# A planned attention-and-long-convolution kernel: the first pair's shared keys apart, zero fills moved, the sine table first, and the last batch's dense units in two sets of banks

## The chip, the cores and the metric

The kernel runs on one core of one Trainium2 chip. The metric is the device time of one launch in microseconds (us), the median of several executions. Five engines work side by side, each in its own program order: TensorE (PE; its weight loads PEld), VectorE (DVE), ScalarE (ACT), GpSimd (POOL) and SyncE (SP), which here only issues DMA.

## What is computed

Eight batches of 448 positions, 12 heads of 64 channels; all inputs and the output are float32.

```python
# attention, with one more exp(-m) in the denominator ("off by one")
scores = q @ k.T / sqrt(64)
e = exp(scores - max); attn = e / (sum(e) + exp(-max) + 1e-9)
x = attn @ v                                   # -> (8, 448, 768), heads side by side
# gate and long convolution
x1, x2, x3 = split(x @ w_proj)                 # w_proj 768 x 2304
x2 = irfft(rfft(x2, axis=1) * rfft(filter, axis=0), n=448, axis=1)
out = (x1 * x2 * x3) @ w_out                   # 768 x 768
```

## The kernel before, in words

Work comes in 48 pairs of heads (six pairs to a batch; index g or i) and, per batch, a dense part. For each pair the keys and queries are turned so that channels lie on partitions, score tiles are made for four blocks of keys (t = 0 to 3), exponentials are taken on ScalarE (`exps`, L652), and the values are weighted (`attn_out`, L684: 28 matmuls in two halves) and normed on VectorE (`norm`, L706). Block 0 of a pair is its *shared* block: the last 64 keys of both heads, laid out as a block diagonal in the tile `ks`; it is made of `rests`, which one DMA loads for a whole batch. Blocks 1 to 3 hold the other keys of each head.

For batches 0 and 1 (`staged`, L300) SP loads keys, values and queries of each pair as float32 into slots of `nat`; the first pair's queries are loaded by ScalarE's queue. GpSimd casts them to bf16 (L343 keys, L349 queries, L356 values; pair 0's queries on VectorE), L372 casts the shared keys into `ks` (for batch 0 half on VectorE, half on GpSimd) and L377 the shared values into `vr`. Then `turn` (L380) transposes the shared block, three key blocks and four query blocks on TensorE into one PSUM bank, and `q_back` and `k_back` (L393, L401) copy the result to `qT` and `kT` on VectorE. Later batches (`loaded`, L418) are loaded and cast by GpSimd's queue and turned by DMA.

The weights are loaded by GpSimd's queue too: the three parts of `wproj_bf` (L626), the filter (L541) and `wout_bf` (L631), each when certain casts have been made (`GATES`, L210).

The dense part of a batch (`dense`, L768) consists of units, each of which fills a PSUM bank on TensorE and is copied out by ScalarE or VectorE:
- P (`proj2`, L822): the x2 projection, on folded x (`xf`), four groups pg by two column halves ch; 6 matmuls each.
- Z (`spectrum`, L849): its transform, two single matmuls per call; VectorE then multiplies with the filter's spectrum (`t`, L866; `yh`, L872).
- G (`gate`, L895): the x1 (part 0) and x3 (part 1) projections of six channel blocks dt, 6 matmuls each; part 0 is copied by ScalarE, part 1 multiplied with it by VectorE (`g`, L913).
- I (`inverse`, L933): the inverse transform of a channel block, 4 matmuls, copied by ScalarE (`cr`, L946); VectorE makes `cw`, `cv` and `yT` of two blocks (L955 to L981).
- O (`project`, L1003): the output projection, 6 matmuls for 128 rows and 384 columns. The first three are split, 4 matmuls on the first four channel blocks and 2 on the last two, so that they can begin before the last `yT` is made.

PSUM holds two score tiles of two banks each (ring `sc`), one attention output (`op`) and three single banks (ring `hy`), which all dense units, the turns and batch 0's shared scores use in turn.

The order on each engine is made by a planner (`Plan`, L42): each step is added with an engine, a cost, a wanted time, what it needs and makes, and which ring slots it takes and gives; `run` simulates the engines and emits each step when its model says that it can start. `after` is a time before which a step may not start in that model. So a changed need, cost or slot moves other steps too. At the start there are small steps of set-up: `spin` (L1087, 40 matmuls on the identity), the fills of `ks` and `vr` with zeros by ScalarE (`blank`, L1084), `phases` and `sines` (L493, L512), which make the tables of the transforms, a first exponential (L1098), and `turn`/`turn_back`, `ft`, `mirror`/`mirror_back` (L550 to L582), which derive the tables bt, ft and fr.

Of the kernel before, what the change touches and what calls it, by code (L numbers as in the profile page):

```python
# [183 lines left out]
def kernel(  # L184
# [21 lines left out]
    BPS = 7.4  # L206
    ZV = 8.0
    RE1 = 4.0
    FT = 7.0
# [90 lines left out]
    def staged(b):  # L300
# [3 lines left out]
        for hp in range(NHP):  # L304
# [62 lines left out]
            if hp == 0:  # L367
                for u in range(2):
                    c = slice(64 * u, 64 * u + 64)
                    on_pool = b > 0 or u == 1  # L370
                    add("POOL" if on_pool else "DVE", 0.55 if on_pool else 0.37, tau(g) - 5.9,
# [8 lines left out]
            def turn(g=g, hp=hp):  # L380
                T[g]["ps"] = tps = phy.tile([128, 512], F32, name="tps", tag="hy")
                tb = tps.bitcast(BF16)
                nc.tensor.transpose(tb[:, 0:128], ks[:, hp, :], ident_bf)
# [9 lines left out]
            def k_back(g=g, hp=hp):  # L393
                tb = T[g]["ps"].bitcast(BF16)
                to = kT[b % 2][:, hp].rearrange("p t c -> p (t c)")
                if g == NHP:
                    nc.scalar.copy(to, tb[:, 0:512])
                else:
                    nc.vector.tensor_copy(to, tb[:, 0:512])
# [8 lines left out]

            w = tau(g) - (3.5 if g else 6.0)
            hy = ("hy", ("T", g))  # L410
            add("PE", 0.45, w, turn, need=[("ck", g), ("cq", g), ("crk", b), "ident"], make=[("T", g)],
# [4 lines left out]
            add(back, 0.36, w + 0.2, k_back, need=[("T", g)] + old, make=[("kT", g)], give=[hy])  # L416
# [130 lines left out]
    def more_tables():  # L547
# [31 lines left out]
        add("PE", 0.25, 24.0, mirror, need=["ft", "half"], make=["rps"], take=[("hy", "rps")])  # L579
# [54 lines left out]
    T = {}  # L634

    def attention(i):
# [27 lines left out]
        for t in range(4):  # L664
            w = tau(i, t / 4)
            ring = "sc" if t or b else "hy"
            if t == 0 or b == 0:
                add("PE", 0.4 if t else 0.19, w, lambda t=t: scores(t),
                    need=[("kT", i), ("qT", i)] + ([("S", i - 1, 2)] if b else []),
# [98 lines left out]
    def dense(b):  # L768
# [5 lines left out]
        at = [0.0]  # L774
# [12 lines left out]
        def xT():  # L787
            return W["xT", b]

# [32 lines left out]
        def proj2(pg, ch):  # L822
            L["P", pg, ch] = pps = phy.tile([128, 512], F32, name="pps2", tag="hy")
# [17 lines left out]
        def P(pg, ch):  # L841
            hy = ("hy", ("P", b, pg, ch))
            w = span(0.97)
            add("PE", 0.975, w, lambda: proj2(pg, ch), need=[("xf", b, pg), ("w", 1)], make=[("P", b, pg, ch)],
# [4 lines left out]
        def spectrum(pg, ch):  # L849
            K = BLK_K[pg]  # L850
            L["Z", pg, ch] = xps = phy.tile([128, 512], F32, name="xsp", tag="hy")
# [25 lines left out]
        def Z(par, ch):  # L877
            xs = ("xs", (b, par, ch))
            for rs in range(2):
                pg = 2 * par + rs  # L880
                hy = ("hy", ("Z", b, pg, ch))
                w = span(0.16)
                add("PE", 0.165, w, lambda pg=pg: spectrum(pg, ch), need=[("x2", b, pg, ch), "ft", ("hrs", par)],
# [11 lines left out]
        def gate(dt, part):  # L895
            L["G", dt, part] = p = phy.tile([128, 512], F32, name="pps1", tag="hy")
# [18 lines left out]
        def G(dt, part):  # L915
            hy, x1 = ("hy", ("G", b, dt, part)), ("x1", (b, dt))
            w = span(1.13)
            add("PE", 1.135, w, lambda: gate(dt, part),
# [250 lines left out]
```

## Time and profile before

| | |
|---|---|
| median of 5 executions | 391.57 us (390.91 to 392.86) |
| profiled execution: own time, span | 391.33 us, 389.5 us |
| mean granted TensorE clock | 0.989 |
| exponentials `e` on ScalarE, 144 of 128x896 | 127.5 us, 924 ns each |
| gates, 576 matmuls of 128x448 (L898) | 121.8 us, 352 ns each |
| `P`, 384 matmuls of 113x384 (L825) | 70.5 us, 326-328 ns each |
| VectorE `g` (L913), 48 | 29.6 us, 616 ns each |
| table loads on ScalarE before 8 us | 3, 1.28 us each |
| `ks` and `vr` zero fills on ScalarE | 0.83 and 0.84 us |
| first scores on TensorE, first exponential | 8.26 us, 8.66 us |
| first P on TensorE | 36.30 us |
| last matmul's end, last copy's end | 384.77 us, 385.27 us |

Times inside a profile count from the start of the span. Matmuls overlap in the pipeline: 352 ns is what one takes from start to end, while the chain counts six of them as 1.14 us. A row of the order of time gives the start, the time taken, the engine, the line, the operation with its tiles, and in brackets how long the engine was idle before it and what ended that. A row of the chain gives start, time, engine and line of a piece of the chain that ended last. A row of the windows gives the stretch, its length, the busy time of PE, PEld, DVE, ACT and POOL, the granted TensorE clock, the DMA share and GB/s.

### The profile page before, as it was taken

The numbers are of one execution on the slowest core, as the hardware profiler recorded it, in microseconds if no ns is written. First come the engines' busy times: TensorE is split into PE (matmuls) and PEld (weight loads), VectorE is DVE, ScalarE is ACT, GpSimd is POOL, SyncE is SP. The second block draws the span as 40 slices with busy tenths as digits, with TensorE's granted clock in tenths as the row PEclk, the third lists the DMA queues.
The fourth block names the chain that finished last, engine by engine and source line by source line (L and its number), as shares of the span: only waits on it lengthen the run. The fifth ranks groups of instructions, "written<-read, shape, count | busy, mean of one in ns | idle before, by whom it ended". The sixth has DMA issues, their size and how long they took to land.

```text
span 389.5 us, 8980 instructions
## 1 busy us (share of the span) xinstructions
PE 373.1 (96%) x3461; PEld 233.8 (60%) x3461; DVE 271.5 (70%) x815; ACT 266.4 (68%) x461; POOL 112.8 (29%) x179
## 2 busy tenths in 40 slices
PE   6997999999999989999999999999999999999895
PEld 5664665656665566556755576556755576566552
DVE  5588769863987559956698449856798449955770
ACT  7797676737776847766876767866876768843443
POOL 7785418436340822331406222601100000000000
PEclk9699999999999999999999999999999999999999
DMA  8999999999999999799999899959831311021004
GB/s 201 245 232 236 223 207 146 154 138 210 144 141 135 234 140 125 98 112 168 137 118 93 156 153 166 86 81 175 116 56 29 140 37 29 15 94 43 0 3 162
DMA packets 179419, 50.44 MB, mean 129 GB/s; under 512 B 166125, under 2 KB 175792, under 8 KB 179376
## 3 DMA queue, kind: packets, MB, share of 16 engines
q0 software_dynamic: 101680, 17.80, 64.6%
q1 hardware_dynamic: 76768, 31.83, 41.6%
q8 instruction: 27, 0.44, 0.5%
q10 hardware_dynamic: 928, 0.23, 0.3%
q14 instruction: 16, 0.13, 0.2%
HBM read 43.86 MB, written 11.01 MB: 141 GB/s over the span
## 4 chain that ended last, share of the span: by engine, by line
PE 86%; DVE 7%; ACT 3%; issue 1%; DMA 1%; POOL 0%; SPq 0%; POOLq 0%; DVEq 0%; ACTq 0%
PE pps L898 27%; PE pps L825 16%; PE ops L1010 14%; PE op L698 9%; PE sc L648 8%; PE op L693 3%; PE cps L937 3%; PE xsp L852 2%; PE sc L650 2%; DMA rests<-in_k_dram 1%; DVE xb L713 1%; ACT e L656 1%; PE xps L747 1%; DVE xf L802 1%; DVE uw L593 1%
## 5 line engine op out<-in xcount | busy, mean ns | idle before, releaser
L656 ACT ACTIVATE e<-sc 128x896 bf16<-128x896 f32 x144 | 127.5, 924 | 17.6 <-PE sc L648 16.6
L898 PE MATMUL pps<-xT,wproj_bf 128*128 128x448 bf16 x576 | 121.8, 352 | 1.1 <-ACT xs L860 0.4
L898 PEld LDWEIGHTS <-wproj_bf 128*128 128x128 bf16 x576 | 52.0, 97 | 47.0 <-issue 7.7
L825 PE MATMUL pps<-wproj_bf,xf 128*113 128x384 bf16 x384 | 70.5, 328 | 0.9 <-ACT xs L860 0.6
L825 PEld LDWEIGHTS <-xf 128*113 128x113 bf16 x384 | 48.5, 132 | 16.6 <-issue 5.7
L698 PE MATMUL op<-vn,e 128*128 128x65 bf16 x1152 | 57.7, 195 | 0.1
L698 PEld LDWEIGHTS <-e 128*128 128x128 bf16 x1152 | 51.2, 98 | 5.6 <-ACT e L656 0.3
L1010 PE MATMUL ops<-wout_bf,yT 128*128 128x384 bf16 x288 | 51.8, 326 | 0.1
L1022 ACT COPY osb<-ops 128x384 f32<-128x384 f32 x56 | 25.9, 484 | 26.9 <-PE ops L1010 26.6
L693 PE MATMUL op<-vr,er 128*128 128x130 bf16 x192 | 42.5, 221 | 1.5 <-DVE xb L713 1.5
L713 DVE TENSOR_TENSOR xb<-op,rec 128x256 bf16<-128x256 f32 x96 | 40.7, 424 | 3.3
L435 POOL DMA_DIRECT2D nat<-in_k_dram x36 | 29.9, 850 | 43.7 <-DMA kT<-nat 42.1
L648 PE MATMUL sc<-qT,kT 64*128 64x448 bf16 x288 | 41.7, 360 | 0.6 <-ACT er L661 0.5
L711 DVE TENSOR_SCALAR rec<-op 128x4 f32<-128x4 f32 x96 | 15.2, 158 | 37.6 <-PE op L698 36.2
L866 DVE TENSOR_TENSOR t<-xs,hrs 113x768 bf16<-113x768 bf16 (+1 forms) x64 | 34.5, 554 | 8.0 <-ACT xs L860 7.8
L910 ACT CAST x<-pps 128x448 bf16<-128x448 f32 x48 | 26.2, 545 | 18.6 <-PE pps L898 17.5
L1010 PEld LDWEIGHTS <-yT 128*128 128x128 bf16 x288 | 26.5, 98 | 19.5 <-DVE yT L981 1.7
L661 ACT ACTIVATE er<-sc 128x448 bf16<-128x448 f32 x48 | 26.7, 557 | 14.3 <-PE sc L650 14.1
L913 DVE TENSOR_TENSOR g<-x,pps 128x448 bf16<-128x448 bf16 x48 | 29.6, 616 | 7.9 <-PE pps L898 7.6
L837 DVE CAST x<-pps 113x384 bf16<-113x384 f32 x32 | 17.8, 555 | 23.4 <-PE pps L825 23.4
L946 ACT CAST cr<-cps 128x452 bf16<-128x452 f32 x48 | 26.3, 549 | 11.4 <-PE cps L937 11.4
L860 ACT CAST xs<-xsp 113x384 bf16<-113x384 f32 (+1 forms) x64 | 28.0, 490 | 5.1 <-PE xsp L852 4.5
(103 smaller groups left out, 440.3 us busy)
## 6 DMA issues: line engine op xcount, KB each, us to landing
out_dram<-osb SPq DMA_DIRECT2D x24, 384.0 KB, 2.3
nat<-in_q_dram POOLq DMA_DIRECT2D x24, 168.0 KB, 5.7
vn<-in_v_dram POOLq DMA_DIRECT2D x6, 672.0 KB, 11.5
wproj_bf<-in_moe_w_proj_dram POOLq DMA_DIRECT2D x3, 1152.0 KB, 12.9
nat<-in_k_dram POOLq DMA_DIRECT2D x36, 96.0 KB, 4.7
nat<-in_q_dram SPq DMA_DIRECT2D x22, 112.0 KB, 5.2
nat<-in_k_dram SPq DMA_DIRECT2D x12, 192.0 KB, 4.5
nat<-in_v_dram SPq DMA_DIRECT2D x12, 192.0 KB, 4.5
```

The lines of the kernel that those rows point to most:

```text
L435: nc.gpsimd.dma_start(kn[:, :, 1 + t, c], kr[:, :, 4 * u + t, :])
L648: nc.tensor.matmul(sc[:, u, 0:S], kT[b % 2][c, hp, t, :], qT[b % 2][c, hp, :])
L656: nc.scalar.activation(e[:, 0 : 2 * S].rearrange("p (u n) -> p u n", u=2), sc[:, :, 0:S], AF.Exp, scale=SCALE)
L693: nc.tensor.matmul(op[:, n, :, :], e[0][:, o : o + 128], vr[b % 2][:, hp, :, :], start=True, stop=False)
L698: nc.tensor.matmul(op[:, n, u, :], e[1 + t][:, u * S + o : u * S + o + 128], vn[b % 2][:, hp, 4 * u + t, :], start=False, stop=(u == 1 and ...
L713: nc.vector.tensor_tensor(W["xb", b][:, hp, 2 * hf : 2 * hf + 2, :].rearrange("p t (u d) -> p t u d", u=2), op[:, :, :, 0:DH], rec[:].unsq ...
L825: nc.tensor.matmul(pps[:FQ, :DCH], W["xf", b][:, pg, kt, 0:FQ], wproj_bf[:, kt, D + ch * DCH : D + (ch + 1) * DCH], start=(kt == 0), stop= ...
L860: nc.scalar.copy(L["xs", par, ch][:K, pg % 2, :], L["Z", pg, ch][:K, :DCH])
L866: nc.vector.tensor_tensor(t[:K], L["xs", par, ch][:K], h, op=ALU.mult)
L898: nc.tensor.matmul(p[:, :S], wproj_bf[:, kt, 2 * part * D + dt * 128 : 2 * part * D + (dt + 1) * 128], xT()[:, kt, 0:S], start=(kt == 0), ...
L913: nc.vector.tensor_tensor(g[:, dt, :], L["x1", dt], p[:, :S], op=ALU.mult)
L1010: nc.tensor.matmul(ops[:n, :DCH], y[:, dt, 0:n], wout_bf[:, dt, ch * DCH : (ch + 1) * DCH], start=(dt == 0), stop=(dt == NDT - 1),)
```

## The change

Six edits, on lines of the kernel before:
- `turn` of pair 0 transposes only the three key and four query blocks; the shared block gets a `turn0` of its own, into its own bank, copied by VectorE (`back0`), while the other key blocks are copied by ScalarE. Pair 0's turn no longer needs the casts of `ks`, and pair 0's shared scores (t = 0) are wanted last of its four.
- The zero fills of `ks` and of `vr[0]` become memsets on VectorE, the second not before 7.4 in the planner's time.
- ScalarE starts with a sine on a dummy value, so that the sine table is loaded first.
- The planner's times for ft, bt (7.0 to 8.0, 7.4 to 8.2) and for `mirror` (24 to 29, and not before) are later.
- The cast of batch 0's shared keys is wanted at 3.0 instead of 0.1.
- In the last batch every other dense unit takes its bank from the score ring instead of the three single banks (`bank`, `room`); of a score tile's two banks one is used.

The planner's new order for these and neighbouring steps follows from that: mirror and the copies `fr` move from the first 12 us behind pair 5's attention, on GpSimd one value cast goes ahead of the first `wproj_bf` load and one cast of shared values behind it, and in the last batch one gate more stands before the first inverse.

```diff
@@ -203,10 +203,10 @@
     BASE2 = 77.0
     READY1 = 80.0
     READY0 = 34.0
-    BPS = 7.4
+    BPS = 8.2
     ZV = 8.0
     RE1 = 4.0
-    FT = 7.0
+    FT = 8.0
     GATES = (
         (1, [("iv", 5), ("ir", 1), ("ik", 7), ("iq", 7)]), ("F", [("cv", 8)]), (0, [("cv", 9)]), (2, [("cv", 10)]),
         ("O", [("cv", 11)]),
@@ -368,7 +368,7 @@
                 for u in range(2):
                     c = slice(64 * u, 64 * u + 64)
                     on_pool = b > 0 or u == 1
-                    add("POOL" if on_pool else "DVE", 0.55 if on_pool else 0.37, tau(g) - 5.9,
+                    add("POOL" if on_pool else "DVE", 0.55 if on_pool else 0.37, tau(g) - 5.9 if g else 3.0,
                         lambda c=c, on_pool=on_pool: (nc.gpsimd if on_pool else nc.vector).tensor_copy(
                             ks[c, :, c], rests[c, 0]
                         ),
@@ -380,7 +380,8 @@
             def turn(g=g, hp=hp):
                 T[g]["ps"] = tps = phy.tile([128, 512], F32, name="tps", tag="hy")
                 tb = tps.bitcast(BF16)
-                nc.tensor.transpose(tb[:, 0:128], ks[:, hp, :], ident_bf)
+                if g:
+                    nc.tensor.transpose(tb[:, 0:128], ks[:, hp, :], ident_bf)
                 for t in range(1, 4):
                     nc.tensor.transpose(
                         tb[:, t * 128 : (t + 1) * 128], T[g]["kn"][:, t - 1, :], ident_bf
@@ -395,8 +396,10 @@
                 to = kT[b % 2][:, hp].rearrange("p t c -> p (t c)")
                 if g == NHP:
                     nc.scalar.copy(to, tb[:, 0:512])
+                elif g:
+                    nc.vector.tensor_copy(to, tb[:, 0:512])
                 else:
-                    nc.vector.tensor_copy(to, tb[:, 0:512])
+                    nc.scalar.copy(to[:, 128:512], tb[:, 128:512])
 
             def q_back(g=g, hp=hp):
                 tb = T[g]["ps"].bitcast(BF16)
@@ -406,14 +409,25 @@
                 else:
                     nc.vector.tensor_copy(to, of)
 
+
+            def turn0():
+                T[0]["ps0"] = tps = phy.tile([128, 512], F32, name="tps0", tag="hy")
+                nc.tensor.transpose(tps.bitcast(BF16)[:, 0:128], ks[:, 0, :], ident_bf)
+
+            def back0():
+                nc.vector.tensor_copy(kT[0][:, 0, 0, :], T[0]["ps0"].bitcast(BF16)[:, 0:128])
+
+            if g == 0:
+                add("PE", 0.1, 2.0, turn0, need=[("crk", 0), "ident"], make=["T0"], take=[("hy", "T0")])
+                add("DVE", 0.2, 2.0, back0, need=["T0"], make=["kT0"], give=[("hy", "T0")])
             w = tau(g) - (3.5 if g else 6.0)
             hy = ("hy", ("T", g))
-            add("PE", 0.45, w, turn, need=[("ck", g), ("cq", g), ("crk", b), "ident"], make=[("T", g)],
+            add("PE", 0.45, w, turn, need=[("ck", g), ("cq", g), "ident"] + ([("crk", b)] if g else []), make=[("T", g)],
                 take=[hy], give=[("k0", g), ("q0", g)])
             old = [("S", g - 2 * NHP, 3)] if b >= 2 else []
             back = "ACT" if g == NHP else "DVE"
             add(back, 0.33, w + 0.1, q_back, need=[("T", g)] + old, make=[("qT", g)], give=[hy])
-            add(back, 0.36, w + 0.2, k_back, need=[("T", g)] + old, make=[("kT", g)], give=[hy])
+            add(back if g else "ACT", 0.36, w + 0.2, k_back, need=[("T", g)] + old, make=[("kT", g)], give=[hy])
 
     def loaded(b):
 
@@ -576,7 +590,7 @@
         add("DVE", 0.35, FT, after=FT, emit=lambda: nc.vector.tensor_scalar(
             ft[:], tab["sb"][:FQ, :, 0:FQ], tab["half"][:FQ, 0:1], None, op0=ALU.mult), need=["sines", "half"],
             make=["ft"])
-        add("PE", 0.25, 24.0, mirror, need=["ft", "half"], make=["rps"], take=[("hy", "rps")])
+        add("PE", 0.25, 29.0, mirror, need=["ft", "half"], make=["rps"], take=[("hy", "rps")], after=29.0)
         add("ACT", 0.9, 25.0, mirror_back, need=["rps"], make=["fr"], take=[("yR", "fr")], give=[("hy", "rps")])
         add("PE", 0.25, BPS, turn, need=["ident", "sines"], make=["bps"], take=[("hy", "bps")], after=BPS)
         add("DVE", 0.7, BPS, turn_back, need=["bps", "half"], make=["bt"], give=[("hy", "bps")])
@@ -662,11 +676,11 @@
 
         P["scores"] = scores
         for t in range(4):
-            w = tau(i, t / 4)
+            w = tau(i, t / 4 if i or t else 1.0)
             ring = "sc" if t or b else "hy"
             if t == 0 or b == 0:
                 add("PE", 0.4 if t else 0.19, w, lambda t=t: scores(t),
-                    need=[("kT", i), ("qT", i)] + ([("S", i - 1, 2)] if b else []),
+                    need=[("kT", i), ("qT", i)] + ([("S", i - 1, 2)] if b else []) + ([] if i or t else ["kT0"]),
                     make=[("S", i, t)], take=[(ring, ("S", i, t))])
             elif (3 * i + t) % 2 == 0:
 
...
@@ -786,6 +800,17 @@
 
         def xT():
             return W["xT", b]
+
+        def bank(key):
+
+            if b == n_batches - 1:
+                at[1] += 1
+            return ("sc" if at[1] % 2 else "hy", key)
+
+        def room(hy, name):
+            if hy[0] == "hy":
+                return phy.tile([128, 512], F32, name=name, tag="hy")
+            return psc.tile([128, 2, 512], F32, name="sc")[:, 0, :]
 
 
         def first(ds, n):
...
@@ -839,16 +864,16 @@
                 nc.scalar.copy(to, of)
 
         def P(pg, ch):
-            hy = ("hy", ("P", b, pg, ch))
+            hy = bank(("P", b, pg, ch))
             w = span(0.97)
-            add("PE", 0.975, w, lambda: proj2(pg, ch), need=[("xf", b, pg), ("w", 1)], make=[("P", b, pg, ch)],
+            add("PE", 0.975, w, lambda: proj2(pg, ch, hy), need=[("xf", b, pg), ("w", 1)], make=[("P", b, pg, ch)],
                 take=[hy], give=[("xf", b)])
             add(("ACT", "DVE")[ch], (0.38, 0.47)[ch], w, lambda: proj2_back(pg, ch), need=[("P", b, pg, ch)],
                 make=[("x2", b, pg, ch)], take=[("x2", b)], give=[hy])
 
-        def spectrum(pg, ch):
+        def spectrum(pg, ch, hy):
             K = BLK_K[pg]
-            L["Z", pg, ch] = xps = phy.tile([128, 512], F32, name="xsp", tag="hy")
+            L["Z", pg, ch] = xps = room(hy, "xsp")
             nc.tensor.matmul(
                 xps[:K, :DCH], ft[:, pg, :K], W["x2", b][:, pg, ch * DCH : (ch + 1) * DCH]
             )
...
@@ -913,9 +938,9 @@
                 nc.vector.tensor_tensor(g[:, dt, :], L["x1", dt], p[:, :S], op=ALU.mult)
 
         def G(dt, part):
-            hy, x1 = ("hy", ("G", b, dt, part)), ("x1", (b, dt))
+            hy, x1 = bank(("G", b, dt, part)), ("x1", (b, dt))
             w = span(1.13)
-            add("PE", 1.135, w, lambda: gate(dt, part),
+            add("PE", 1.135, w, lambda: gate(dt, part, hy),
                 need=[("xT", b, h) for h in range(NHP)] + [("w", 2 * part)] + ([("G", b, dt - 2, 1)] if dt > 1 and not part else []),
                 make=[("G", b), ("G", b, dt, part)], take=[hy])
             if part == 0:
...
@@ -1081,9 +1106,6 @@
         add("DVE", 0.2, -19.5, number, need=["count"], make=["row"])
         add("DVE", 2.6, -19.0, phases, need=["row"], make=["phases"])
 
-        def blank(to):
-            nc.scalar.copy(to, zero1[0 : to.shape[0], :].to_broadcast(list(to.shape)))
-
         def spin():
 
             t = phy.tile([128, 512], F32, name="spin", tag="hy")
@@ -1091,10 +1113,11 @@
                 nc.tensor.matmul(t[:, 0:128], ident_bf, ident_bf)
 
         add("PE", 4.0, -20.0, spin, need=["ident"], make=["spin"], take=[("hy", "spin")], give=[("hy", "spin")])
-        add("ACT", 1.6, -20.0, lambda: blank(ks[:].rearrange("p g c -> p (g c)")), need=["zero1"], make=["zero ks"])
-
-        add("ACT", 0.8, -18.0, lambda: blank(vr[0][:].rearrange("p g u d -> p (g u d)")), need=["zero1"], make=[("zero vr", 0)])
-        add("ACT", 0.6, -17.0, sines, need=["phases"], make=["sines"])
+        add("DVE", 0.7, -18.0, lambda: nc.vector.memset(ks, 0.0), need=["phases"], make=["zero ks"])
+
+        add("DVE", 0.7, 5.0, lambda: nc.vector.memset(vr[0], 0.0), make=[("zero vr", 0)], after=7.4)
+        add("ACT", 1.3, -20.0, lambda: nc.scalar.activation(warm, zero1, AF.Sin), need=["zero1"], make=["sine table"])
+        add("ACT", 0.6, -19.0, sines, need=["phases"], make=["sines"])
         add("ACT", 1.5, -16.0, lambda: nc.scalar.activation(warm, zero1, AF.Exp), need=["zero1", "sines"])
 
         def pads():
```

The hunks left out do to `proj2`, `spectrum`, `inverse`, `project` and the functions that plan them what the two shown do to `P` and to `gate`: the ring slot comes from `bank` and the tile from `room`.

## The prediction, made before the changed kernel was run

> **What bounds the kernel now.** I read the page's engine rows first, then the chain that ended last, then the order of time of its two ends, since the change touches only the first 36 us and the last batch.
>
> ```profile
> PE 373.1 (96%) x3461; PEld 233.8 (60%) x3461; DVE 271.5 (70%) x815; ACT 266.4 (68%) x461; POOL 112.8 (29%) x179
> ...
> PE 86%; DVE 7%; ACT 3%; issue 1%; DMA 1%; POOL 0%; SPq 0%; POOLq 0%; DVEq 0%; ACTq 0%
> ```
>
> TensorE is busy 96% of the span and carries 86% of the chain. Its idle time is 16.4 us; by the windows 7.8 us lie before 60 us and 4.7 us behind its last matmul, so from 60 us on, lost TensorE time is lost for good and won time is kept. The chain of the last batch, in order of time, shows where TensorE waits there:
>
> ```profile
> 357.56 0.49 ACT x L839
> ...
> 359.43 0.49 ACT xs L860
> ...
> 362.27 0.49 ACT xs L860
> ...
> 368.39 0.63 DVE g L913
> ```
>
> Each is the evacuation of a dense unit's bank: with three banks the fourth unit waits for the first to be copied out. With a fifth at 364.13 (x, L910) the chain leaves TensorE for 0.55 + 0.56 + 0.55 + 0.60 + 0.77 = 3.03 us. VectorE in the same stretch, in order of time:
>
> ```profile
> 369.53 0.40 DVE L955 TENSOR_TENSOR cw<-cr 128x452 bf16<-128x452 bf16 x1 [0.53 <-ACT cr L946]
> ...
> 374.59 0.61 DVE L913 TENSOR_TENSOR g<-x,pps 128x448 bf16<-128x448 bf16 x1
> ...
> 376.99 0.62 DVE L913 TENSOR_TENSOR g<-x,pps 128x448 bf16<-128x448 bf16 x1 [0.34 <-PE pps L898]
> 377.64 0.56 DVE L981 TENSOR_TENSOR yT<-g,cv 128x768 bf16<-128x768 bf16 x1
> ```
>
> From 369.53 on VectorE has hardly a gap, and its last yT ends at 378.20, only 0.64 us before TensorE needs it (378.84, below). In the head, GpSimd's rows and the clock by windows:
>
> ```profile
> 20.60 0.50 POOL L343 CAST k<-nat 128x384 bf16<-128x384 f32 x1 [2.14 <-PE xps L747]
> 21.04 0.50 POOL L377 CAST vr<-rests 64x384 bf16<-64x384 f32 x1
> 21.76 0.61 POOL L349 CAST q<-nat 112x512 bf16<-112x512 f32 x1 [0.22 <-PE op L698]
> 22.32 1.06 POOL L626 DMA_DIRECT2D wproj_bf<-in_moe_w_proj_dram  x1
> ```
>
> ```profile
> 5.97:9.38 3.41, 1.88 (x21) 1.01 (x17) 2.20 (x7) 2.77 (x5) 3.23 (x16) 0.98 1.23 256
> 9.38:12.79 3.41, 3.08 (x16) 1.28 (x14) 1.17 (x4) 3.38 (x6) 3.22 (x8) 0.50 1.19 275
> ```
>
> The key cast at 20.60 is pair 5's. The page puts its wait down to a transpose, but the buffer that it refills had been read by 17.1; its load was issued at 14.61 and took 5.8 us, so it landed at 20.4. The queries of pair 5 (21.76) likewise follow their load (issued from 15.66, 5.4 us). GpSimd then runs without a break to 26.3, where pair 6 gets its last keys: loads, not arithmetic, pace this stretch. The clock column (0.98, then 0.50) shows TensorE at half rate after a window with 1.88 us of work.
>
> **The last batch, step by step.** Every other dense unit takes a score bank: five banks for three. No work is added or removed. Per unit the chain shows P 0.98, a pair of spectra 0.34, a gate G 1.14, an inverse 0.21. From 357.54 (five P done) without waits: 4 spectra pairs 1.36, 3 P 2.94, 5 gates 5.70 give the first inverse at 367.54. The new order has one gate more before it than the old. Six inverses and the other four gates then end at 374.50, against 376.88: 2.4 us, not 3.03, because 0.65 of the gaps is spectra running inside them.
>
> But the output needs VectorE. Three half projections (12 matmuls, 1.96) precede the first that needs the last yT: 376.88 + 1.96 = 378.84 before, 376.46 if only TensorE counted. VectorE: gate 4's x copy on ScalarE ends at 368.1, two inverse copies (0.97 a pair) 369.07, so cw starts at 369.1, only 0.4 before the old 369.53. From cw to g at 374.59 the old rows take 5.06; about 0.2 of that was a wait for a gate (371.81). So g ends at 374.6, cw and cv (1.43) 376.0, g 0.65, yT 0.56: 377.2. Projections resume at 377.25 instead of 378.84: **1.6 us gained**, 0.8 less than TensorE alone would give. The bank of the first projection, released by g at 374.6, costs 0.1 inside this. Bounds: 1.0 if ScalarE brings the inverses no earlier than now, 2.4 if VectorE keeps up. The work behind is the same 5.93 us of matmuls, one copy and the store. Copies out of the score banks I take at the price of the exp er of the same bank, 0.55, against 0.53 for the x copy: no change.
>
> **The head.** ScalarE loses two fills (0.83 + 0.84) and one of three table loads, gains a 0.20 sine warm-up and the copy of pair 0's three key blocks (not shown; nearest a 448 copy on ScalarE, 0.55): free at about 6.1 instead of 8.05. That cover was not the limit: ScalarE waited 0.61 for the first scores. [...] VectorE gains the two fills; a memset of 780 takes 0.71 (L1113). The ks fill lies in its idle 1.78 us before 5.73, though at 3.95 it precedes pair 0's query cast; the vr fill lies after 7.3, with nothing due until pair 1's copies near 9.7. Bounds 0.35 to 0.71 each, and no cost. Pair 0's turn no longer waits for GpSimd's ks cast (6.79) and starts behind the spin at 6.14; the shared block turns by itself near 6.9. That turn waits for both ks casts with the first scores queued behind it on TensorE, but these wait for kT until 7.25 anyway. First scores about 7.25 instead of 8.26, first exp 1.0 us earlier, and the fr copies (0.92) leave ScalarE's early stream, to come back near 33 between exponentials of pair 6, which delays those by 0.9; ScalarE has nothing at all in 38 to 40, so I cost that at nothing.
>
> What of it arrives at 36 us? Pair 5 is turned at 22.4 at the earliest (query cast 22.37), against 22.65: 0.25 remains. GpSimd's new order puts pair 5's vn cast (0.65) ahead of the first wproj issue and one vr cast (0.50) behind. So the issue goes from 22.32 to about 23.0, and 12.9 later the weights land at 35.9 or 36.0 instead of 35.2. The first projection P started at 36.30; now it starts at 36.0, but four score matmuls (0.48) that stood before it come after it. Net 36.0 + 0.48 - 36.30 = +0.2, against 0.47 us of TensorE idle in 44 to 50 that may shrink. I take **zero**, bounds -0.5 and +0.7. SP's order changes in one batch only (one kT transpose moved behind an xT one), where the half of a pair's output moves before a gate on TensorE; it is a second half, whose exponentials the first half has had, so I cost it at nothing.
>
> [...]
>
> Sum on the profiled execution: span 389.5 - 1.6 = 387.9, own time 391.33 - 1.6 = 389.7; that execution lies 0.24 below the median 391.57, so the median becomes **390.0**.
>
> **Rivals.**
> 1. Likeliest, 0.45: tail -1.6, head 0: 390.0, itself 389.0 to 391.0.
> 2. Both ends gain, 0.25: some 1.5 of the head survives (later loads follow earlier casts) or VectorE keeps up: 388.5. [...] Against: pair 5's loads.
> 3. It does not do what it says, 0.17: the wproj issue lands 1.2 late and gives back the tail: 391.2. For it: other weight loads took 13.7 and 18.2 us.
> 4. Slower, 0.13: one place, the first P at 36.0. If its weights land after about 37, TensorE, its scores now behind P, has under 1.9 us of work in the window 33.3 to 36.7 (2.47 now) and falls to half clock as at 9.4; two windows cost 3.4, the late start 1.2: 391.57 - 1.6 + 4.6 = 394.6. Against: the window 29.9 to 33.3 had 2.24 and kept its clock.
>
> A measurement tells about 0.3% (1.2 us) from no change: faster means under 390.4, slower over 392.7. Faster 0.25 + 0.7 of 0.45 = 0.56; same 0.31; slower 0.13. The range leaves out rival 4 and the end of rival 2: 388.0 to 391.9.
>
> **What would show it.** Right: no TensorE waits on bank copies in the last batch, projections starting near 374.5 (shifted by the head), and one wait of about 0.7 for yT; first exp near 7.7; pair 5's key cast still at 20.6; wproj issued near 23 and P at 36. Wrong: a key cast of pair 5 well before 20; P before 35; a clock of 0.5 after 33; projections without a wait for yT, or gates still waiting.

## The result and the profile after

The changed kernel takes 389.56 us (median of 43 runs, 387.52 to 392.77) against 391.06 for the kernel before (80 runs, 388.54 to 395.61): ratio 0.9960, 95% interval 0.9947 to 0.9974, a gain of 1.5 us. The forecast was 390.0, a gain of 1.6 on the 391.57 that five runs of the kernel before had given. The profiled execution took 391.69 us (span 389.9), 2.1 above the median, so it is read by stretches and not by its end. Ratios leave out executions more than 1.5% above the fastest of their kernel, among them two of tail_alone's twelve, 393.39 and 393.78, with which its mean would stand at 0.995 of the kernel before's instead of 0.993.

The page of the changed kernel, engine rows and the chain by engine:

```profile
PE 372.7 (96%) x3461; PEld 234.0 (60%) x3461; DVE 270.5 (69%) x817; ACT 264.4 (68%) x460; POOL 114.0 (29%) x179
...
PE 80%; DVE 8%; DMA 4%; ACT 3%; issue 2%; POOL 1%; SPq 1%; POOLq 0%; DVEq 0%; ACTq 0%
```

The engines do what they did. The chain has less of TensorE, partly since it runs through VectorE at the end, partly through a transfer that was late in this execution. The last batch, in order of time (all engines):

```profile
371.29 0.40 DVE L980 TENSOR_TENSOR cw<-cr 128x452 bf16<-128x452 bf16 x1 [1.88 <-ACT cr L971]
...
375.96 0.61 DVE L938 TENSOR_TENSOR g<-x,sc 128x448 bf16<-128x448 bf16 x1
...
377.84 0.61 DVE L938 TENSOR_TENSOR g<-x,pps 128x448 bf16<-128x448 bf16 x1
...
378.49 0.56 DVE L1006 TENSOR_TENSOR yT<-g,cv 128x768 bf16<-128x768 bf16 x1
...
379.10 0.50 PE L1035 MATMUL sc<-wout_bf,yT 128*128 128x384 bf16 x2 [0.36 <-DVE yT L1006]
```

The five waits for copies of banks are gone; one wait of 0.36 us, for the last yT, is left. To size the gain, take from the chain the start of the last batch's four transposes (xps) and the start of the last copy (osb), in the kernel before and then in the changed one:

```profile
350.15 0.22 PE xps L747 x4
...
384.79 0.48 ACT osb L1022
```

```profile
352.52 0.22 PE xps L761 x4
...
385.16 0.48 ACT osb L1047
```

Between the two it is 32.64 us instead of 34.64: **the last batch gained 2.0 us**. That stretch hardly varies: in six other profiles with the new banks and this order it is 32.62 to 32.64, and in two others with the old ones 34.63.

The head, GpSimd in order of time:

```profile
20.45 0.50 POOL L343 CAST k<-nat 128x384 bf16<-128x384 f32 x1 [2.22 <-PE xps L761]
20.90 0.61 POOL L349 CAST q<-nat 112x512 bf16<-112x512 f32 x1
21.49 0.64 POOL L356 CAST vn<-nat 128x192 bf16<-128x192 f32 x2
24.16 1.06 POOL L640 DMA_DIRECT2D wproj_bf<-in_moe_w_proj_dram  x1 [2.03 <-issue]
...
27.05 0.50 POOL L343 CAST k<-nat 128x384 bf16<-128x384 f32 x1
```

Pair 5's keys are cast at 20.45, as before (20.60). But the weights' issue comes at 24.16 instead of 22.32, after 2.03 us in which GpSimd waited for nothing that the profile names, and pair 6's key cast at 27.05 instead of 25.83. TensorE turns these keys 1.2 us later (kernel before, then changed kernel):

```profile
26.39 0.34 PE L385 MATMUL tps<-ident_bf,k 128*128 128x128 bf16 x3 [0.30 <-POOL k L343]
```

```profile
27.61 0.34 PE L386 MATMUL tps<-ident_bf,k 128*128 128x128 bf16 x3 [0.34 <-POOL k L343]
```

The first yT of batch 0, a mark that all kernels share, comes 1.1 us later (again before, then changed):

```profile
71.25 0.55 DVE L981 TENSOR_TENSOR yT<-g,cv 128x768 bf16<-128x768 bf16 x1
```

```profile
72.37 0.56 DVE L1006 TENSOR_TENSOR yT<-g,cv 128x768 bf16<-128x768 bf16 x1
```

So **the head lost about 1 us**. The rest of this execution's lateness is its own: TensorE waited 1.62 us at 248.17 behind a transfer of xT that took 6.58 us to land. It is one of the transposes whose order on SP the change moved, but in the eight other profiles with that order this transfer took 2.9 to 3.8 us, and TensorE has no idle time between 240 and 252 us.

### The profile page after: what moved, and what is told of

Same layout as the page of the kernel before. It is cut to its first block, busy times and chain, and to the rows that moved or that the text cites. A ratio compares the mean times of both kernels' runs of the same rounds, so it can differ in the third digit from the quotient of the medians.

```text
span 389.9 us, 8977 instructions
## 1 busy us (share of the span) xinstructions
PE 372.7 (96%) x3461; PEld 234.0 (60%) x3461; DVE 270.5 (69%) x817; ACT 264.4 (68%) x460; POOL 114.0 (29%) x179
## 4 chain that ended last, share of the span: by engine, by line
PE 80%; DVE 8%; DMA 4%; ACT 3%; issue 2%; POOL 1%; SPq 1%; POOLq 0%; DVEq 0%; ACTq 0%
PE pps L923 22%; PE pps L850 15%; PE ops L1035 11%; PE op L712 8%; PE sc L662 8%; PE op L707 3%; PE xsp L877 2%; PE cps L962 2%; PE sc L664 2%; DMA xT<-xb 2%; DMA kT<-nat 1%; PE sc L923 1%; DVE g L938 1%; DMA nat<-in_q_dram 1%; DVE cv L991 1%
## 5 line engine op out<-in xcount | busy, mean ns | idle before, releaser
L923 PE MATMUL pps<-xT,wproj_bf 128*128 128x448 bf16 x522 | 110.6, 352 | 1.9 <-DVE g L938 1.8
L850 PE MATMUL pps<-wproj_bf,xf 128*113 128x384 bf16 x360 | 66.9, 328 | 0.6 <-DMA wproj_bf<-in_moe_w_proj_dram 0.2
L1035 PE MATMUL ops<-wout_bf,yT 128*128 128x384 bf16 x270 | 49.3, 326 | 0.3 <-DVE yT L1006 0.2
L725 DVE TENSOR_SCALAR rec<-op 128x4 f32<-128x4 f32 x96 | 15.2, 158 | 39.6 <-PE op L712 38.4
L1047 ACT COPY osb<-ops 128x384 f32<-128x384 f32 x52 | 24.2, 484 | 23.2 <-PE ops L1035 23.0
L935 ACT CAST x<-pps 128x448 bf16<-128x448 f32 x42 | 22.9, 546 | 15.3 <-PE pps L923 12.6
L938 DVE TENSOR_TENSOR g<-x,pps 128x448 bf16<-128x448 bf16 x45 | 27.7, 616 | 8.0 <-PE pps L923 7.7
L885 ACT CAST xs<-xsp 113x384 bf16<-113x384 f32 (+1 forms) x60 | 26.6, 491 | 3.8 <-PE xsp L877 3.2
```

Source lines behind the costliest of these rows:

```text
L850: nc.tensor.matmul(pps[:FQ, :DCH], W["xf", b][:, pg, kt, 0:FQ], wproj_bf[:, kt, D + ch * DCH : D + (ch + 1) * DCH], start=(kt == 0), stop= ...
L923: nc.tensor.matmul(p[:, :S], wproj_bf[:, kt, 2 * part * D + dt * 128 : 2 * part * D + (dt + 1) * 128], xT()[:, kt, 0:S], start=(kt == 0), ...
L938: nc.vector.tensor_tensor(g[:, dt, :], L["x1", dt], p[:, :S], op=ALU.mult)
L1035: nc.tensor.matmul(ops[:n, :DCH], y[:, dt, 0:n], wout_bf[:, dt, ch * DCH : (ch + 1) * DCH], start=(dt == 0), stop=(dt == NDT - 1),)
```

## The experiments

Twelve kernels, each timed in five rounds beside the kernel before (12 executions each, 8 of no_shared1). In the table, "head" and "last batch" say whose edits a kernel has; "first yT" and "last batch us" (from xps to the last copy, as above) come from its profile; * marks profiles with a stretch of half clock between 20 and 46 us.

| kernel | head | last batch | ratio to before, 95% interval | first yT | last batch us |
|---|---|---|---|---|---|
| after | new | new | 0.9960, 0.9947 to 0.9974 | 72.37 | 32.64 |
| tail_alone | old | new | 0.9931, 0.9898 to 0.9964 | 73.89* | 32.63 |
| head_alone | new | old | 1.0017, 0.9990 to 1.0045 | 72.33 | 34.63 |
| own_bank | new, one edit | new | 0.9981, 0.9956 to 1.0005 | 71.79 | 32.62 |
| weights_ahead | new, one move | new | 0.9968, 0.9938 to 0.9999 | 72.59* | 32.63 |
| two_more | new, no stall | new | 0.9961, 0.9927 to 0.9995 | 75.76* | 32.63 |
| one_fewer | old, with stall | old | 1.0025, 0.9998 to 1.0053 | 72.12 | 34.63 |
| keys_first | as two_more, other loads | new | 1.0004, 0.9973 to 1.0034 | 73.64* | 32.64 |
| no_shared1 | new, two loads less | new | 0.9936, 0.9905 to 0.9967 | 71.28 | 32.64 |
| remainder_pool | new | new, yR on GpSimd | 1.0010, 0.9987 to 1.0033 | 71.95 | 33.2 |
| remainder_last | new | same, order kept | 0.9965, 0.9933 to 0.9997 | 72.69 | 32.66 |
| tail_and_remainder | old | same, order kept | 0.9956, 0.9923 to 0.9988 | 70.88 | 32.67 |
| remainder_after | old | new, yR last | 0.9957, 0.9922 to 0.9992 | 71.31 | 32.40 |

**Which end made the gain.** tail_alone is the kernel before with `bank` and `room` alone; head_alone is the changed kernel with

```diff
         def bank(key):
-            if b == n_batches - 1:
-                at[1] += 1
             return ("sc" if at[1] % 2 else "hy", key)
```

> The kernel before with only the banks of the last batch changed; the head is that of before. Theory (the whole gain is made in the last batch, as forecast, only somewhat larger than the 1.6 us of the forecast): 389.0 to 389.6 against 391.1 for before, that is 1.5 to 2.1 us; in its profile 32.6 us from the last batch's shared transposes (xps) to the end of the last matmul, instead of 34.6, no waits for copies of banks, one wait of about 0.4 for the last yT. Rival (the gain comes from the head, the last batch only trades one wait for another): 390.8 to 391.3, and over 34 us in that stretch.

> The changed kernel with the three single banks in the last batch as before; only the edits of the head are left. Forecast: no change against before (391.1; bounds -0.5 and +0.7). Theory after the trace: 0.3 to 0.9 slower than before, because GpSimd's issue of the weights comes 1.8 us later and pair 6's casts with it; the first scores near 7.9 and the first exponential near 8.3 change nothing of that. Rival (the head is where the gain is): 389.6.

Measured: tail_alone 0.9931 (391.06 x 0.0069 = 2.7 us, interval 1.4 to 4.1), with 32.63 us in the last batch; head_alone 1.0017 (+0.7 us, interval -0.4 to +1.8). The gain is made in the last batch, and the head keeps part of it. That the head is slower in time is likely but not shown by its interval alone; the first yT says it too. Among the profiles without half clock after 20 us it comes at 71.25, 70.88 and 71.31 with the old head, at 72.37, 72.33, 71.79, 71.95 and 72.69 with the new: means 71.15 and 72.23, 1.1 us apart, in groups that do not overlap. These are single profiles, one of each kernel.

**Pair 0's copies.** The queries of pair 0 get a bank of their own:

```diff
+                if not g:
+                    T[g]["psq"] = phy.tile([128, 512], F32, name="tpsq", tag="hy")
+                    tb = T[g]["psq"].bitcast(BF16)
                 for j in range(NST):
```

> The changed kernel with pair 0's queries turned into a bank of their own, so that VectorE's copy of the queries and ScalarE's copy of the keys no longer read one bank. Theory: the two copies ran one after the other because they share a bank; now they run side by side, first scores at 7.3 to 7.5 instead of 7.88, first exponential 0.4 to 0.5 earlier, near 7.8; the total stays within 0.3 us of the changed kernel (389.6), since the loads of pair 5 set the pace behind. Rival 1: the copies still run one after the other (something other than the bank), first scores 7.9. Rival 2: the earlier start comes through to the end, 389.1 or less.

The two copies, in order of time, in the changed kernel and in own_bank:

```profile
6.92 0.48 ACT L402 COPY kT<-tps 128x384 bf16<-128x384 bf16 x1 [0.84 <-PE tps L390]
7.43 0.39 DVE L410 COPY qT<-tps 128x448 bf16<-128x448 bf16 x1 [1.41 <-ACT kT L402]
```

```profile
6.65 0.48 ACT L405 COPY kT<-tps 128x384 bf16<-128x384 bf16 x1 [0.57 <-PE tps L386]
7.02 0.39 DVE L413 COPY qT<-tpsq 128x448 bf16<-128x448 bf16 x1 [1.06 <-PE tpsq L393]
```

In the changed kernel VectorE waits for ScalarE's copy (which ends at 7.40; VectorE's starts at 7.43), in own_bank for TensorE's transposes. The one edit between the two is the second bank, and with it that wait is gone. Then the copies overlap (6.65 to 7.13 and 7.02 to 7.41), scores start at 7.47 instead of 7.88, and the time does not fall (0.9981). The earlier start bought nothing.

**The stall ahead of the weights.** First, the issue is moved ahead of pair 5's value cast in the planned order, nothing else:

```diff
         self.order = order
+        a = next(i for i, (_, t) in enumerate(order) if ("w", 1) in t[6])
+        z = next(i for i, (_, t) in enumerate(order) if ("cv", 5) in t[6])
+        order.insert(z, order.pop(a))
```

> The changed kernel with one instruction moved: GpSimd issues the first part of the projection weights ahead of pair 5's value cast instead of behind it, as in the kernel before; every other engine's order is the same. Theory (the late issue, at 24.2 instead of 22.3, is what the head loses): issue near 21.5 to 22.5 with no stall ahead of it, P no longer waits for weights, pair 6's key cast 1 us earlier, 0.4 to 1.0 us faster than the changed kernel: 388.6 to 389.2. Rival (the stall of 2.0 us belongs to the issue wherever it stands, or is chance): the stall moves with it, or pair 6's casts stay where they are, and the time stays 389.3 to 389.9.

The stall moves with it (1.68 us, issue at 23.30), no gain: 0.9968. Next, its cause. The DMA queues hold packets of kind "instruction". The row of queue 14 (packets, MB, share of the engines' time) in the stretch 18 to 19 us of the kernel before, and in 22 to 23 us of the changed one:

```profile
q14 instruction: 1, 0.01, 3.4%
```

```profile
q14 instruction: 1, 0.01, 2.2%
```

Before, this packet of 8 KB runs from 18.35 to 18.89, most of it inside GpSimd's idle time ahead of pair 5's keys (18.45 to 20.60). In the changed kernel it runs from 22.22 to 22.58, behind that wait, and the weights are issued after it, at 24.16. GpSimd's program has 68 instructions ahead of that wait before, and 67 after. So two kernels shift that count and hardly anything else, one from each side:

```diff
 # two_more, from the changed kernel (69 ahead of the wait)
-            for u in range(2):
+            for u in range(2 + 2 * i):
+                u %= 2
                 nc.gpsimd.memset(vr[i][64 * u : 64 * u + 64, :, u, DH : DH + 1], 1.0)
 # one_fewer, from the kernel before (67 ahead of it)
-            for e in er:
-                nc.gpsimd.memset(e[:, S:], 0.0)
+            nc.gpsimd.memset(er[0][:, S:], 0.0)
+            nc.vector.memset(er[1][:, S:], 0.0)
```

> The changed kernel with two of GpSimd's small memsets (the ones of vr for batch 1, 64x6, near 17.8) issued twice, so that everything behind them stands two instructions later in GpSimd's program; nothing else moves. Theory: the stall of 2.0 us ahead of the weights' issue is a fetch of GpSimd's instructions. In the kernel before it comes near 18.5 and lies inside the wait for pair 5's keys (2.1 us); in the changed kernel GpSimd has one instruction less ahead of that wait, so the fetch comes behind it, near 22.4, with the weights waiting. With two more memsets the packet of the instruction queue comes back to 18 to 19, the weights are issued near 22.1 without a stall, pair 6's key cast ends 1 to 2 us earlier, and the time is 0.5 to 1.0 us under the changed kernel (389.6): 388.6 to 389.1. Rival (the stall has another cause, such as the loads that fill the DMA queues): the issue stays at 23.3 to 24.2, time unchanged.

> The other way round: the kernel before with one of GpSimd's small memsets (the pad of er, 128x32) given to VectorE, so that GpSimd has one instruction less ahead of its wait for pair 5's keys; all else stands as before. Theory (instruction fetch): the fetch moves from near 18.5 to behind that wait, 21 to 22.5, and the weights' issue stalls 1.5 to 2 us (23.5 to 24.2 instead of 22.3); 0.4 to 1.0 us slower than before. Rival (the stall comes from what the change does at the start): issue near 22.3 without a stall, same time as before.

GpSimd in order of time, two_more and then one_fewer:

```profile
20.16 0.50 POOL L343 CAST k<-nat 128x384 bf16<-128x384 f32 x1 [0.34 <-DMA nat<-in_k_dram]
...
22.41 1.07 POOL L640 DMA_DIRECT2D wproj_bf<-in_moe_w_proj_dram  x1
```

```profile
20.72 0.51 POOL L343 CAST k<-nat 128x384 bf16<-128x384 f32 x1 [2.48 <-PE sc L648]
...
23.99 1.07 POOL L626 DMA_DIRECT2D wproj_bf<-in_moe_w_proj_dram  x1 [1.76 <-issue]
```

Both go as the fetch theory says: the stall vanishes from the new head (packet at 19.8 to 20.1 us) and appears in the old one (packet from 21.9 to 22.6). A cause in the start of the kernel is excluded, since one_fewer has the old start. In time one_fewer is 1.0 us slower (interval -0.1 to +2.1), its first yT 0.87 us later: the size of the head's loss. two_more turns pair 6's keys at 26.28, as the kernel before did (26.39), but in twelve executions it is no faster than the changed kernel (0.9961), so the 0.5 to 1.0 us that I expected did not come. In its profile the weights still land only at 35.8 (TensorE waits 1.51), and GpSimd then waits 7.55 us for pair 8's queries, so TensorE loses 2.58 us at 41.2. That the stall goes with the place of this packet is thus shown from both sides; that the packet is a fetch of GpSimd's instructions is the author's reading of the queue's name and of the count. That the stall is what the head loses in time is shown from one side only, and why two_more does not win it back stays open. In the changed kernel the packet itself took 0.36 us of a stall of 2.03; what the rest waits for is not shown. From 12.7 to 36.0 us of the changed kernel the DMA engines' share is 1.12, at 242 GB/s. The stall was 1.3 to 2.4 us in the eight profiles with 67 instructions ahead of pair 5's keys (in one of them, remainder_pool, the row names a load as its end), and nothing in the six with 68 or 69.

**What paces the head.** keys_first changes SP's order in two_more: the two shared loads of batch 1 go behind pair 5's keys and queries. no_shared1 leaves those two loads out of the changed kernel.

```diff
 # keys_first
         self.order = order
+        a = [x for x in order if ("rv", 1) in x[1][6] or ("rk", 1) in x[1][6]]
+        for x in a:
+            order.remove(x)
+        z = next(i for i, (_, t) in enumerate(order) if ("sq", 5) in t[6])
+        order[z + 1 : z + 1] = a
 # no_shared1
-                        lambda name=name, x=x: nc.sync.dma_start(rests[:, "kv".index(name)], shared(x, b)),
+                        lambda name=name, x=x: b or nc.sync.dma_start(rests[:, "kv".index(name)], shared(x, b)),
```

> The kernel two_more with SP's order changed as well: batch 1's two shared loads (1.7 us of SP's time from 12.7 on) go behind the loads of pair 5's keys and queries. Theory (the loads of pair 5 set the pace of the head, so that its earlier start is lost): pair 5's key cast near 18.8 to 19.5 instead of 20.4, the weights issued near 21 to 21.5, and 0.5 to 1.2 us faster than two_more. Rival (the head is paced by something behind it, such as GpSimd's casts of pair 6 or the weights' landing): pair 5 comes earlier, but the first yT of batch 0 and the total are as in two_more within 0.3 us.

> The changed kernel without the two loads of batch 1's shared keys and values (2 x 192 KB near 12.7 to 14.5); the casts then take batch 0's, so that batch 1's attention is computed from other data. Nothing else moves. Theory (the bytes that are loaded in the first 45 us set the pace of the head, whatever is issued first; that is why an earlier start, a weights' issue without a stall and keys ahead of the shared loads all gave nothing): the DMA engines move some 240 KB a us there, so 384 KB less is 1.0 to 1.6 us, of which 0.7 to 1.6 comes through: pair 5's key cast near 19, and 388.0 to 388.9. Rival (something else paces the head: GpSimd's casts, or TensorE at half clock): 389.3 to 389.9.

Another order gives nothing: in keys_first pair 5's keys landed near 18.7 instead of 20.0 in two_more, but GpSimd had pair 4's queries to cast first (18.24; 17.85 in two_more), and pair 5's keys were cast at 20.28 (20.16) and the weights issued at 22.57; 1.0004. So my expectation of 18.8 to 19.5 failed. In no_shared1 these keys landed at 18.3, and GpSimd's own work, in order behind pair 4's queries, held them up too:

```profile
17.85 0.62 POOL L349 CAST q<-nat 112x512 bf16<-112x512 f32 x1 [1.27 <-DMA nat<-in_q_dram]
...
19.82 0.50 POOL L343 CAST k<-nat 128x384 bf16<-128x384 f32 x1 [0.34 <-POOL vr L1134]
```

So the cast came at 19.82 and not near 19, and the stall is there (2.17 us). Still the first yT comes at 71.28, 1.1 us earlier than in the changed kernel and 0.5 earlier than in the earliest other profile with the new head; 0.9936. 384 KB at the changed kernel's 242 GB/s is 1.6 us of transfer, an estimate. When the weights were issued did not decide when they landed: issued at 22.4 to 23.6 in two_more, keys_first, head_alone and no_shared1, they landed at 35.6 to 35.8 in all four. That fewer bytes help is likely and not shown. It rests on the first yT of one profile; leaving the loads out also takes 1.7 us off SP's issuing; P begins at 35.84, but in head_alone, which has the same head with all its loads, at 35.63; and the intervals in time overlap.

**What bounds the last batch now.** If VectorE's chain from the first cw to the last yT does, work taken off it must show. First the yR products of the last batch go to GpSimd:

```diff
-            nc.vector.tensor_tensor(y, W["g", b][:, ds, c], L["cv", dp][:, :, c], op=ALU.mult)
+            e = nc.gpsimd if n and b == n_batches - 1 else nc.vector
+            e.tensor_tensor(y, W["g", b][:, ds, c], L["cv", dp][:, :, c], op=ALU.mult)
```

> The changed kernel with the three yR products of the last batch (0.22 us each on VectorE) given to GpSimd; the planner then also puts one yR projection ahead of the first half that needs the last yT. Theory (VectorE's chain cw, cv, g, yT sets when the projections resume in the last batch): last yT 0.3 to 0.4 us earlier against the first inverse, TensorE's wait of 0.36 for it is gone, 32.6 from the last batch's xps to the last matmul's end becomes 32.2 to 32.3; in the time 0.2 to 0.4, which is near what can be told. Rival (TensorE alone bounds the last batch now, the wait is only for show): 32.6 stays; or GpSimd's products come late and the yR projections wait: 33 or more.

Here the planner put a yR projection and its stores ahead. The last matmul ended 32.3 us behind xps, but a full store of 384 KB was then the last one issued, behind two short ones (SP's queue in order of time):

```profile
383.15 1.12 SPq L1058 DMA_DIRECT2D out_dram<-osb  x2
384.36 0.54 SPq L1055 DMA_DIRECT2D out_dram<-osb  x1
```

From xps to the end of the span it is 38.4 us instead of 37.4, and the time is 1.0010. About half of that is the store, which ended 4.8 us behind the last copy instead of 4.3; the other half is ScalarE, which waited 2.39 us for the last matmul and then had three copies left. So the order was held in the next two, by a need of the last projections:

```diff
+            if st == 3 and b == n_batches - 1:
+                need += [("O", b, 2, 1)]
```

> As remainder_pool (the last batch's yR products on GpSimd), but the yR projections are held behind the others, so that TensorE's, ScalarE's and SP's orders are those of the changed kernel. Theory (what remainder_pool lost came from the order of the stores: its last full store of 384 KB was issued behind the two short ones and ended the program 4.8 us after the last copy instead of 4.3): last yT 0.3 us earlier, projections resume without or with under 0.1 us of wait, 32.2 to 32.4 from the last batch's xps to the last matmul's end, 37.0 from there to the end of the span instead of 37.4, time 389.1 to 389.4. Rival (GpSimd's products beside VectorE slow its chain, or reach the last projections late): 32.6 or more, time 389.6 or more.

> The kernel tail_alone (head of the kernel before, new banks in the last batch) with the yR products of the last batch on GpSimd, projections in order as in remainder_last: the best of what was seen. If the gains of the last batch add: 2.3 us under before, 388.5 to 389.0, ratio near 0.994. If the GpSimd products give nothing: as tail_alone, 388.9 to 389.4.

The store's loss is gone (0.9965), but the last batch still takes 32.66. VectorE in order of time:

```profile
374.37 0.62 DVE L980 TENSOR_TENSOR cw<-cr 128x452 bf16<-128x452 bf16 x1
374.91 0.60 DVE L938 TENSOR_TENSOR g<-x,sc 128x448 bf16<-128x448 bf16 x1
```

Its chain takes 7.79 us (7.76 in the changed kernel) although two products left it: a cw beside GpSimd's product (373.94 to 374.74) takes 0.62 instead of 0.40 (0.62 to 0.63 in the three kernels with products on GpSimd). The place of that cw is new too, and a g and the yT beside GpSimd's products kept their 0.61 and 0.56, so contention is one reading and not isolated. tail_and_remainder, with the old head, is the same in the last batch (32.67) and 0.9956 in time. The last kernel keeps the products on VectorE, behind the last yT:

```diff
         self.order = order
+        a = [x for x in order if any(k[:3] == ("y", 7, 1) for k in x[1][6] if isinstance(k, tuple))]
+        for x in a:
+            order.remove(x)
+        z = next(i for i, (_, t) in enumerate(order) if ("y", 7, 0, 2) in t[6])
+        order[z + 1 : z + 1] = a
```

> The kernel tail_alone with the last batch's yR products left on VectorE but moved behind its last yT (one cv of that batch lies in the dead tile nat, so that no buffer is missing); only VectorE's order differs. Theory (VectorE's chain from the first cw to the last yT sets when the projections resume; remainder_last gained nothing because GpSimd's product beside it stretched a cw from 0.40 to 0.62 and took back what it saved): the chain from the first cw to the end of the last yT falls from 7.76 to 7.4 to 7.5 us, TensorE's wait for it from 0.36 to under 0.1, and from the last batch's xps to the last matmul's end it is 32.3 us instead of 32.6; time 0.3 under tail_alone, ratio to before 0.992 to 0.995. Rival (TensorE bounds the last batch, or another wait takes the place): 32.6 stays.

TensorE in order of time:

```profile
378.62 0.50 PE L1037 MATMUL sc<-wout_bf,yT 128*128 128x384 bf16 x2 [0.16 <-DVE yT L1008]
```

The chain falls to 7.52, the wait to 0.16, the stretch to 32.40: 0.24 us for 0.24 us taken off VectorE. So VectorE's chain sets the end of the last batch. In time (0.9957) that can't be told from tail_alone. The three kernels with the old head and the new banks lie at 0.9931 to 0.9957, under the changed kernel by no more than their intervals; by the profiles, old head and remainder_after's last batch are the best of each end.

## Why the prediction was right, and where not

**The last batch: mechanism right, the size 0.4 too small.** Waits for copies disappear, the inverses start earlier, VectorE is next, one wait for yT remains: all as forecast. The mis-sized term is VectorE's chain. I let cw start at 369.1 and the last yT end at 377.2, 8.1 us. It took 7.76 (8.67 before), since all of the old rows' gaps went, 0.91 us; I took out 0.2 of them by name and some 0.35 more by setting the last rows end to end. The first cw came 0.6 us earlier against xps instead of 0.4, the two inverse copies counting 0.89 and not 0.97. The wait for yT was 0.36, not 0.7. (Behind the first inverse there are five gates, not "the other four"; the sum of 374.50 has five.)

**The head: the size "zero" failed, at the step "So the issue goes from 22.32 to about 23.0".** It went to 24.16, and pair 6 and P followed (P at 36.65 instead of 36.0). I added the value cast that goes ahead of the issue (0.65) and did not see the packet on the instruction queue, which with one instruction less came behind GpSimd's wait for pair 5's keys (at 22.22 instead of 18.35); the cast ahead of the issue ended at 22.13, so the rest is the stall. The loss, about 1 us by the profiles and 0.7 by head_alone, is at the upper bound of +0.7 or past it. How much of it the stall makes is open, as two_more shows. So 390.0 is close partly by luck: two errors, 0.4 and about 1, have opposite signs; 1.6 and 0 were each off. By the profiles 2.0 less about 1 is 1.0, the low end of what was measured (1.0 to 2.1).

**"Loads, not arithmetic, pace this stretch" was right.** Pair 5's key cast stayed at 20.45, though the first exponential came 0.38 us earlier (8.28 instead of 8.66). The 1.5 us that rival 2 let the head gain are in no run; it lost about 1. Nor did the clock decide anything. In the kernel before half rate (0.50) stood from 9.25 to 16.08 us (6.83 us, half of which is the 3.4 that rival 4 counts), behind 3.41 us with 1.89 of TensorE work. It came in the changed kernel too, from 10.06 to 16.88, behind 3.41 us with 1.59 of work. In head_alone it did not come, and nothing was won by that: its profile shows no half rate in the head at all. Windows (stretch, length, PE, PEld, DVE, ACT, POOL busy, granted clock, DMA share, GB/s):

```profile
5.97:9.38 3.41, 1.91 (x22) 1.13 (x19) 2.21 (x6) 2.18 (x4) 2.66 (x13) 1.00 1.22 263
9.38:12.79 3.41, 2.47 (x41) 1.72 (x42) 1.48 (x7) 2.80 (x5) 3.22 (x10) 1.00 1.18 281
```

Its first yT comes at 72.33, the changed kernel's at 72.37 with half rate from 10.1 to 16.9. From 5.97 to 16.20 TensorE was busy for 7.44 us there, for 7.88 in the changed kernel: full clock only made it idle more.

**First scores at 7.25**: 7.88, and the first exponential at 8.28 instead of near 7.7. The two copies that I ran side by side read one bank, and there VectorE's waited for ScalarE's (7.43 against 7.02 with a bank of its own). I had compared orders, not waits. By own_bank it cost nothing that the time shows.

**Rival 3 came nearest on the head** (weights late), but gave back half of the gain and not all. **Rival 4's price exists, but not in the changed kernel's profile**: half rate between 35 and 46 us stands in three of the twelve other kernels' profiles (tail_alone 37.7 to 41.1, keys_first 35.9 to 39.3, two_more 41.8 to 45.2), one of them with the old head. keys_first comes near the rival's picture: scores behind P, a wait of 1.05 us for the weights, and 1.93 us of work in the 3.41 ahead of the half rate. But the bound of 1.9 us of work, under which the rival let the clock fall, is the author's estimate from one row, and the kernel before goes against it: from 28.40 to 31.81 us TensorE had 1.60 us of work, and the clock stayed at 1.00 there and behind it. In tail_alone TensorE had waited 1.44 us for a cast of queries. There, 12 P matmuls took 3.78 us, against 2.16 in the kernel before:

```profile
37.76 3.78 PE L844 MATMUL pps<-wproj_bf,xf 128*113 128x384 bf16 x12
```

That is 1.6 us for one stretch of 3.4, and may be part of why single runs scatter over 5 us. **SP's moved transpose** at no cost was right by the eight other profiles with that order.

## What to carry to other kernels

Price the two ends of a kernel by different clocks: where transfers filled the DMA engines (share 1.12 from 12.7 to 36.0 us of the changed kernel), an earlier start (own_bank, 0.9981), another order (keys_first, 1.0004) or a faster clock (head_alone, 1.0017) gave nothing here, and only leaving bytes out seemed to (no_shared1, 0.9936); where one batch drains at the end, more banks moved the bound to the next engine's chain, and all of its gaps went (8.67 us, then 7.76). Read the waits of a built program and not its order alone. A "waited for nothing" of 1.3 to 2.4 us ahead of an instruction went here with a packet of the instruction queue: look for such a packet, and shift the stream by one or two instructions to see it move.

## What was unexpected of the hardware

- One instruction more or less in GpSimd's program ahead of its wait for pair 5's keys went with a stall of 1.3 to 2.4 us behind that wait, or with none, in all fourteen profiles as the count says (67, or 68 and 69). The 8 KB packet of the instruction queue began at 18.35 us (before) and 19.8 (two_more) where there was no stall, and at 22.22 (the changed kernel) and 21.9 (one_fewer) where there was one.
- The stretches of half clock start at another place in each of these executions of nearly the same program, and differ in length: 6.83 us from 9.25 (before) and from 10.06 (the changed kernel), 3.4 us from 37.7 (tail_alone) and from 41.8 (two_more), and nowhere in the head of head_alone. How busy TensorE was in the 3.41 us ahead does not decide it alone: in the kernel before, 1.89 us (5.83 to 9.25) was followed by half rate, while the clock stayed at 1.00 behind 1.60 us (28.40 to 31.81). Why the start moves is not shown.
